# Block attention and MoE layer on one core: the column softmax's weights turned on VectorE instead of TensorE, sread in 32x64 tiles

## The chip, the cores and the metric

The kernel runs on one core of a Trainium2 chip. The metric is device time in microseconds of one execution; the median of three runs is given. A profile shows one execution of the program.

## The reference

Two stages are chained. The first is an attention between 512 tokens `x` and 32 state rows per head, for 8 batches of 8 heads with 64 elements. The scores are used twice: a softmax along the states (rows) gives `xread`, a softmax along the tokens (columns) gives `sread`.

```python
# x: (8, 8, 512, 64), state: (8, 8, 32, 64), all float32
scores = scale * x @ state^T                      # 512 x 32
xread  = softmax(scores, -1) @ state              # 512 x 64
scores2 = scale * state @ x^T                     # 32 x 512
sread  = softmax(scores2, -1) @ x                 # 32 x 64
attn = concatenate([xread, sread], axis=2)        # 544 rows per batch and head
# second stage, on rows of H*D = 512 elements
h = attn_rows @ w_in                              # 512 -> 2048
r = maximum(h, 0); g = s * (r * r) + b
out = g @ w_out                                   # 2048 -> 512, 4352 rows
```

## The kernel before, in words

There are no loops over stages. `ORDER` (lines 15 to 75) is a list of words, and lines 713 to 716 emit the piece that each word names, in that order, on the engine that the piece uses. An argument `V`, `A` or `G` puts a piece on VectorE (DVE), ScalarE (ACT) or GpSimd (POOL). Each engine works its own instructions strictly in this order, so a piece whose input is late holds back everything behind it on its engine. DMAs of inputs are issued from POOL's queue (x, weights; line 217 to 220 from ACT, line 214 from SyncE), those of outputs from SyncE's.

A batch b (8 of them, number 0 in two halves p at the start) goes through these pieces:

- `x` (load_x, L177): both head groups g of four heads, tokens laid out so that a partition holds 16 successive tokens of a head, converted to 16 bits. `xn` (load_xn, L188): the same data in a second layout for sread. Batch 0 comes as `xf` by SyncE in four parts (L210) and is cast by `castx`.
- `xT` (L283): DVE turns 32x32 blocks. `T` (L291): the scores by 16 matmuls of 32x32 weight tiles and 512 columns. `U`, `mu`, `D`, `E1`, `z`, `At`, `A` (L312 to 358): the row softmax, whose result `A` is again turned on DVE.
- `M` (L423) multiplies the states with w_in, eight matmuls of 64x32 tiles for each quarter j; `Mc` copies it to SBUF. So layer 1 of xread is `l` or `lh` (L469, L473): two matmuls of 512 columns with `M` and `A`, then a relu on ACT. `s`, `sh` square it.
- `L` (L492), a quarter of layer 2 for 128 rows: four matmuls of 512 columns; `out` adds the bias and stores. Batches 5 to 7 use a Strassen-like scheme instead: sums `S` of blocks, 14 half products `P`, evictions `ev`, stores `put`.
- The column softmax: `nm`, `nms` (maximum over the tokens), `E2` (L374, exp on ACT), `a2` (L381, scaling by the reciprocal sum on DVE, written in another order of the tokens). `aps` (L391) turns it with eight TensorE transposes of 128x128 into PSUM, `a2T` (L397) copies that to SBUF on ACT or DVE, and `V` (L400) multiplies with `xn`: 32 matmuls of 128x64 weights and 32 columns a batch, one PSUM bank, two batches together in two of the calls. `srd` (L420) copies the result to `srdT` on ACT.
- At the end `lsr`, `ssr`, `S_sr`, `P_sr`, `ev_sr` do both layers for the sread rows of all batches.

PSUM has eight banks: two rooms of two banks (`two_banks`, L130: `ps_t` with own=1, `ps_a` with own=0), which `T`, `M`, `aps`, `V` and a few others take in turn, two single banks for layer 1 and two for layer 2. `idle` (L656) are matmuls on constants at the start. All small matmuls go through the helper `mm` and so have line L137 in the profile.

Of the kernel before, what the change touches and what calls it, by code (L numbers as in the profile page):

```python
# [78 lines left out]
def kernel(  # L79
# [90 lines left out]
    srdT = konst.tile([P, NK, Ns, B], FP16, name="srdT")  # L170
# [5 lines left out]

    def load_x(b):  # L177

        if b > 2:
            nc.gpsimd.tensor_copy(ahead, at[b - 1]["xT"][0:1, 0, 0])  # L180
        xh_t[b] = xpool.tile([P, NG, NT, D], FP16, name=f"xh_{b}", tag="xh")
        for g in range(NG):
            nc.gpsimd.dma_start(
                out=xh_t[b][:, g].rearrange("p j d -> p (j d)"),
                in_=x[b, 4 * g : 4 * g + 4].rearrange("r (t j) d -> (r t) (j d)", j=NT),
            )

    def load_xn(b):  # L188

        xn_t[b] = xpool.tile([P, H, SCH, D], FP16, name=f"xn_{b}", tag="xn")  # L190
        for jh in range(4):
            nc.gpsimd.dma_start(  # L192
                out=xn_t[b][32 * jh : 32 * jh + 32].rearrange("t h c d -> t h (c d)"),
                in_=x[b].rearrange("h (t jh c) d -> jh t h (c d)", t=32, jh=4)[jh],
            )
# [15 lines left out]
    for p in range(2):  # L211
        for g in (1, 0):
            h = slice(NT // 2 * p, NT // 2 * p + NT // 2)
            nc.sync.dma_start(
                xf[g][:, h], x[0, 4 * g : 4 * g + 4].rearrange("r (t j) d -> (r t) j d", j=NT)[:, h]
            )
# [174 lines left out]
    def at_aps(b):  # L391
        at[b]["aps"] = aps = blocks(two_banks(f"aps_{b}", FP16), 0)
        for g in range(NG):
            for c in range(SCH):
                transp(aps[:, SCH * g + c], at[b]["a2"][:, g, P * c : P * c + P])
# [351 lines left out]
```

## Time and profile before

| | |
|---|---|
| median of 3 runs | 224.83 us (224.76 to 225.58) |
| the profiled execution | 224.36 us |
| its span in the profile | 222.2 us |
| instructions in the profile | 4473 |
| granted TensorE clock | full speed in all 40 slices |
| DMA | 22.67 MB in 23416 packets |
| `l`: two matmuls of 512 columns, then the relu (L456) | 0.61 us on ACT |
| copy `srdT` (L421), 128x128 | 0.73 us on ACT (median) |
| `a2` (L385), 128x512 | 0.35 us on DVE |
| `A` turned (L353), 128x512 pairs | 0.71 us on DVE |
| `aps` copied (L152) | 1.02 us on ACT, 0.67 us on DVE |
| square of 128x1024 | 0.68 us on DVE, 1.08 us on ACT |
| product of 128x512 on POOL (L462) | 1.06 us |

An engine's busy time is the time in which at least one of its instructions ran; a matmul's duration contains its latency, so that successive matmuls overlap and what one costs is read from start to start. PE is TensorE's matmuls, PEld its weight loads, L the line of the kernel, and a name such as `vps<-a2T,xn` says which tile is written from which.

### The profile page before, as it was taken

Reading aid. Unit: us, or ns where it says so; the run is one execution under the profiler, and the core shown is the slowest. Engines: PE = TensorE matmul, PEld = TensorE weight load, DVE = VectorE, ACT = ScalarE, POOL = GpSimd, SP = SyncE. Lnnn points to the kernel's source line nnn. Section 1 sums busy time; section 2 is a strip of 40 time slices with the busy share of each in tenths; the row PEclk is TensorE's granted clock in tenths of the full one; section 3 lists DMA queues with packets and bytes.
Section 4 is the critical chain, followed back from the end, with each engine's and each line's share of the span. In section 5 each row is a group of like instructions: output and inputs, shape, how many; then the busy total and the mean of one; then the engine's idle time right before and its main releaser. Section 6 shows DMA issues by size and latency. Waiting matters only on the chain.

```text
span 222.2 us, 4473 instructions
## 1 busy us (share of the span) xinstructions
PE 210.7 (95%) x1816; PEld 115.8 (52%) x1816; DVE 183.6 (83%) x267; ACT 141.8 (64%) x243; POOL 43.4 (20%) x73
## 2 busy tenths in 40 slices
PE   6469999999999999999999999999999999999992
PEld 2234334444444443444454544457766778888881
DVE  1597998889769997989796799889999997966772
ACT  2475895776488869855787479485877858533400
POOL 8245504000273400046002160005200000000000
PEclk9999999999999999999999999999999999999999
DMA  6999993420557892048927397226903500440066
GB/s 158 227 207 206 205 193 58 101 72 20 100 112 117 112 174 50 16 100 120 192 47 133 96 128 124 49 45 101 141 2 65 127 0 3 94 99 0 3 134 149
DMA packets 23416, 22.67 MB, mean 102 GB/s; under 512 B 4196, under 2 KB 16996, under 8 KB 23396
## 3 DMA queue, kind: packets, MB, share of 16 engines
q0 software_dynamic: 16560, 12.26, 38.6%
q1 hardware_dynamic: 6160, 9.97, 18.2%
q8 instruction: 14, 0.23, 0.4%
q10 hardware_dynamic: 676, 0.16, 0.3%
q14 instruction: 6, 0.05, 0.1%
HBM read 25.72 MB, written 8.91 MB: 156 GB/s over the span
## 4 chain that ended last, share of the span: by engine, by line
PE 88%; DMA 4%; DVE 3%; ACT 3%; SPq 1%; issue 0%
PE ops L496 31%; PE hps L452 24%; PE opf_X L137 9%; PE opf_W L137 5%; PE mps L137 4%; DMA xf<-in_x_dram 4%; PE hps_sr L452 3%; PE opf_Y L137 2%; PE vps L137 2%; PE T_None L137 2%; PE aps L137 2%; PE ops_sr_X L137 2%; ACT M L152 1%; DVE xT L289 1%; PE ops_sr_W L137 1%; ACT rh L482 1%
## 5 line engine op out<-in xcount | busy, mean ns | idle before, releaser
L456 ACT ACTIVATE r<-hps 128x512 f16<-128x512 f32 x120 | 69.3, 610 | 29.8 <-PE hps L452 28.4
L496 PE MATMUL ops<-w_out,g 128*128 128x512 f16 x320 | 78.1, 379 | 1.3 <-DVE g L462 1.3
L452 PE MATMUL hps<-A,M 128*128 128x512 f16 x240 | 65.3, 380 | 0.5 <-DVE M L152 0.3
L496 PEld LDWEIGHTS <-g 128*128 128x128 f16 x320 | 30.3, 98 | 38.4 <-issue 2.8
L462 DVE TENSOR_TENSOR g<-r 128x1024 f16<-128x1024 f16 (+1 forms) x39 | 34.5, 897 | 8.1 <-ACT r L456 8.0
L452 PEld LDWEIGHTS <-M 128*128 128x128 f16 x240 | 21.9, 98 | 25.8 <-issue 4.7
L137 PEld LDWEIGHTS <-g 128*128 128x128 f16 x288 | 28.0, 98 | 6.4 <-issue 0.2
L152 ACT CAST M<-mps 128x1024 f16<-128x1024 f32 x28 | 28.0, 1013 | 1.8 <-PE mps L137 1.8
L192 POOL DMA_DIRECT2D xn<-in_x_dram x32 | 18.5, 588 | 29.2 <-PE vps L137 28.3
L506 DVE SCALAR_TENSOR_TENSOR osb<-ops,sb_bc,bias_bc 128x512 f32<-128x512 f32 x20 | 14.7, 734 | 1.0 <-PE ops L496 1.0
L180 POOL COPY ahead<-xT 1x2 f16<-1x2 f16 x5 | 1.8, 367 | 67.0 <-DVE xT L289 67.0
L456 ACT ACTIVATE r_sr<-hps_sr 128x256 f16<-128x256 f32 x16 | 6.2, 385 | 12.8 <-PE hps_sr L452 12.4
L564 DVE TENSOR_TENSOR g<-g 128x1024 f16<-128x1024 f16 x18 | 12.2, 685 | 2.0 <-PE opf_Y L137 1.9
L289 DVE STREAM_TRANSPOSE xT<-xh 128x1024 f32<-128x1024 f32 (+2 forms) x12 | 10.3, 871 | 3.2 <-ACT xh L152 3.2
L333 DVE TENSOR_REDUCE z<-E 128x32 f32<-128x1024 f16 (+1 forms) x9 | 9.9, 1095 | 3.7 <-ACT E L328 3.7
L137 PE MATMUL opf_X<-w_T,g 128*128 128x256 f16 x96 | 11.9, 273 | 0.0
L137 PE MATMUL mps<-w_in,stT 64*32 64x512 f16 x256 | 11.2, 383 | 0.2 <-ACT M L152 0.2
L318 DVE TENSOR_REDUCE mu<-U 128x32 f32<-128x1024 f32 (+1 forms) x9 | 9.9, 1097 | 0.2
L376 ACT ACTIVATE E<-T_None,nms 128x512 f16<-128x512 f32 x8 | 5.5, 691 | 6.9 <-DVE nms L372 4.4
L328 ACT ACTIVATE E<-Dm 128x1024 f16<-128x1024 f32 (+1 forms) x9 | 8.7, 963 | 1.8 <-DVE Dm L322 1.5
L322 DVE TENSOR_TENSOR Dm<-U,mu 128x1024 f32<-128x1024 f32 (+1 forms) x8 | 9.6, 1201 | 0.2
L314 DVE STREAM_TRANSPOSE U<-T_None 128x1024 f32<-128x1024 f32 x7 | 8.7, 1247 | 1.2 <-PE T_None L137 0.8
(94 smaller groups left out, 259.4 us busy)
## 6 DMA issues: line engine op xcount, KB each, us to landing
out_dram<-osb SPq DMA_DIRECT2D x32, 128.0 KB, 2.7
xn<-in_x_dram POOLq DMA_DIRECT2D x32, 128.0 KB, 5.7
xh<-in_x_dram POOLq DMA_DIRECT2D x14, 256.0 KB, 5.2
out_dram<-osx SPq DMA_DIRECT2D x24, 128.0 KB, 2.4
w_in<-in_moe_w_in_dram POOLq DMA_DIRECT2D x8, 256.0 KB, 10.6
w_out<-in_moe_w_out_dram POOLq DMA_DIRECT2D x4, 512.0 KB, 12.7
xf<-in_x_dram SPq DMA_DIRECT2D x4, 256.0 KB, 7.5
out_dram<-osb SPq DMA_DIRECT2D x4, 256.0 KB
```

The lines of the kernel that those rows point to most:

```text
L137: return nc.tensor.matmul(out, lhsT, rhs, start=start, stop=stop, tile_position=tp, is_transpose=is_transpose, skip_group_check=skip,)
L152: (engine.copy if engine is nc.scalar else engine.tensor_copy)(out, in_)
L192: nc.gpsimd.dma_start(out=xn_t[b][32 * jh : 32 * jh + 32].rearrange("t h c d -> t h (c d)"), in_=x[b].rearrange("h (t jh c) d -> jh t h (c ...
L289: nc.vector.transpose(part(out, p, g), part(in_, p, g))
L318: nc.vector.tensor_reduce(part(mu, p), blk(part(at[b]["U"], p)), AX.X, ALU.max)
L333: nc.vector.tensor_reduce(part(z, p), blk(part(at[b]["E1"], p)), AX.X, ALU.add)
L452: nc.tensor.matmul(hps, lhsT, rhs, start=(i == 0), stop=(i == len(terms) - 1))
L456: nc.scalar.activation(R_t[tag, q][:, i], hps, AF.Relu)
L462: e.tensor_mul(g, r, r)
L496: nc.tensor.matmul(ops_t[tag, rr], G_t[tag][:, f, P * rr : P * rr + P], w_out_f(f), start=(f == 0), stop=(f == NKF - 1),)
L506: nc.vector.scalar_tensor_tensor(osb, ops_t.pop((tag, rr)), s_bc, bias_bc, ALU.mult, ALU.add)
L564: e.tensor_tensor(out, x, y, op)
```

## The change

The two copies of a batch's tokens are laid out anew. `x_u` splits the 512 tokens into halves u of 256; a partition holds eight successive tokens of each half (four DMAs a batch for two). `xn` gets the layout that the first copy had: 16 successive tokens of a head in a partition, in three DMAs for four. `T` reads its columns in the order (v u t), so that the scores and all that follows from them for the column softmax are in that order, and `a2` writes straight on. `aps` is gone; `a2T` is one DVE instruction that turns 32x32 blocks of pairs within SBUF. `V` has 128 matmuls a batch: 16 steps j, in each the eight tiles of 32 rows by 64 columns (four row groups hp, two column groups g), which write into four banks, that is both rooms. `srd` copies from the two rooms with one instruction each, to an `srdT` whose last axis is now the states. The output's row patterns follow the new layouts. Pieces may take a whole (index 2 of `HALVES`) where they took a half, tiles for the relu's results are given out in turn, and `ORDER` is written anew throughout, with other engines for many pieces.

```diff
 ORDER = [
-    "win.0 win.1 wout.0 x.1 win.2 wout.1 win.3 wout.2 wout.3 idle.11 castx.1.0.V castx.0.0.A xT.0.0.0 "
-    "casts.A turn.0.4.A pair.0.4 xT.0.1.0 T.0.1.0 U.0.0 mu.0.0 sb castx.1.1.A castx.0.1.A D.0.V.0 "
-    "xT.0.0.1 idle.6 xT.0.1.1 E1.0.0 T.0.0.1 keep.0.0 M.0.0.1 Mc.0.0.A z.0.0 At.0.V.0 A.0.0 idle.4 "
...
+    "x.1 casts.V pair.0.4 castx.0.0.V castx.1.0.A xT.0.0.0 turn.0.4.A xT.0.1.0 T.0.1.0 U.0.0 mu.0.0 "
+    "D.0.V.0 castx.1.1.A xT.0.1.1 E1.0.0 castx.0.1.V xT.0.0.1 keep.0.0 idle.8 win.0 M.0.0.1 z.0.0 "
+    "Mc.0.0.A T.0.0.1 keep.0.1 idle.4 win.1 idle.2 At.0.V.0 A.0.0 U.0.1 lh.0.2.0 mu.0.1 wout.0 D.0.V.1 "
+    "lh.0.0.0 M.0.1.0 Mc.0.1.A win.2 E1.0.1 win.3 sh.0.2.0.V M.1.0.1 sb Mc.1.0.A lh.0.4.0 lh.0.6.0 "
...
+    "L.2.0.2 l.2.15 l.2.14 L.2.3.0 L.2.3.1 l.3.2 l.3.5 V.3 srd.3 l.3.3 s.2.14.2.G L.2.0.3 out.2.0 l.3.8 "
...
+    "out.2.1 V.4 srd.4 l.3.4 s.3.4.4.V T.5.1 l.3.12 l.3.11 nm.5 s.3.0.4.A L.2.3.2 L.2.2.0 nms.5.A L.2.2.1 "
...
+    "L.3.2.2 L.3.2.3 out.3.2 V.2 s.4.2.2.V srd.2 l.4.14 V.5 srd.5 L.3.3.3 l.4.10 l.4.15 out.3.3 s.4.0.2.V "
...
-    srdT = konst.tile([P, NK, Ns, B], FP16, name="srdT")
+    srdT = konst.tile([P, NK, B, Ns], FP16, name="srdT")
+    def x_u(b, g, u):
+        return x[b, 4 * g : 4 * g + 4].rearrange("r (u t v) d -> u r t v d", u=2, t=32)[u]
...
-        for g in range(NG):
+        for g, u in np.ndindex(NG, 2):
             nc.gpsimd.dma_start(
-                out=xh_t[b][:, g].rearrange("p j d -> p (j d)"),
-                in_=x[b, 4 * g : 4 * g + 4].rearrange("r (t j) d -> (r t) (j d)", j=NT),
+                out=xh_t[b][:, g, NT // 2 * u : NT // 2 * u + NT // 2].rearrange("p v d -> p (v d)"),
+                in_=x_u(b, g, u).rearrange("r t v d -> r t (v d)"),
             )
...
-        for jh in range(4):
+        for g, k, n in ((0, 0, 4), (1, 0, 2), (1, 2, 2)):
+            h = 4 * g + (k ^ 2 * g)
             nc.gpsimd.dma_start(
-                out=xn_t[b][32 * jh : 32 * jh + 32].rearrange("t h c d -> t h (c d)"),
-                in_=x[b].rearrange("h (t jh c) d -> jh t h (c d)", t=32, jh=4)[jh],
+                out=xn_t[b][32 * k : 32 * k + 32 * n, g].rearrange("p j d -> p (j d)"),
+                in_=x[b, h : h + n].rearrange("r (t j) d -> (r t) (j d)", j=NT),
             )
...
+    def in_order(t, p, turned):
+        if p is not None:
+            return t
+        if turned:
+            return t.rearrange("q (u v t) -> q v u t", u=2, t=32)
+        return t.rearrange("q (v u t) -> q v u t", u=2, t=32)
     def at_T(b, own=1, p=None):
...
-                    r = hp ^ g
+                    r = hp ^ 2 * g
                     mm(
-                        part(T[Ns * hp : Ns * hp + Ns], p, g)[:, 0, :],
+                        in_order(part(T[Ns * hp : Ns * hp + Ns], p, g)[:, 0, :], p, False),
                         stE[32 * r : 32 * r + 32, NG * b + g, :, e],
-                        part(at[b]["xT"][32 * r : 32 * r + 32, :, :, e], p, g)[:, 0, :],
+                        in_order(part(at[b]["xT"][32 * r : 32 * r + 32, :, :, e], p, g)[:, 0, :], p, True),
...
-            nc.vector.tensor_scalar(
-                a2[:, g].rearrange("p (c jh t) -> p jh c t", c=4, jh=4),
-                at[b]["E2"][:, g].rearrange("p (jh c t) -> p jh c t", c=4, jh=4),
-                q[:, g : g + 1], None, ALU.mult,
-            )
-    def at_aps(b):
-        at[b]["aps"] = aps = blocks(two_banks(f"aps_{b}", FP16), 0)
-        for g in range(NG):
-            for c in range(SCH):
-                transp(aps[:, SCH * g + c], at[b]["a2"][:, g, P * c : P * c + P])
-    def at_a2T(b, e):
-        copy(e, sm(b, "a2T", [P, NG * SCH, P], FP16, apool, 2), at[b]["aps"])
-    def at_V(*bs):
-        pair = two_banks(f"vps_{bs[0]}")
...
+            nc.vector.tensor_scalar(a2[:, g], at[b]["E2"][:, g], q[:, g : g + 1], None, ALU.mult)
+    def at_a2T(b):
+        a2T = sm(b, "a2T", [P, NG, NT // 2, Ns, 2], FP16, apool, 2)
+        nc.vector.transpose(
+            a2T.rearrange("p g v n e -> p (g v n e)").bitcast(FP32),
+            at[b]["a2"].rearrange("p g s -> p (g s)").bitcast(FP32),
+        )
+    def at_V(b):
+        pair = at[b]["vps"] = [two_banks(f"vps_{b}_{i}", own=i) for i in range(2)]
+        a2T, xn = at[b]["a2T"], xn_t[b]
+        for j in range(NT):
+            e, v = j // (NT // 2), j % (NT // 2)
+            for hp in range(4):
                 for g in range(NG):
...
+                    r, rows = hp ^ 2 * g, slice(32 * hp, 32 * hp + 32)
+                    mm(
+                        pair[r // 2][D * g : D * g + D, r % 2, :Ns],
+                        xn[rows, g, j, :],
+                        a2T[rows, g, v, :, e],
+                        start=(j == 0),
+                        stop=(j == NT - 1),
+                        tp=(32 * hp, D * g),
+                    )
     def at_srd(b):
-        nc.scalar.copy(srdT[:, :, :, b], at[b]["vps"])
+        for i in range(2):
+            nc.scalar.copy(srdT[:, 2 * i : 2 * i + 2, b], at[b]["vps"][i][:, :, :Ns])
```

More of the change, by code (lines that the diff above doesn't have):

```diff
@@ L181, in load_x @@
         xh_t[b] = xpool.tile([P, NG, NT, D], FP16, name=f"xh_{b}", tag="xh")
-        for g in range(NG):
+        for g, u in np.ndindex(NG, 2):
             nc.gpsimd.dma_start(
-                out=xh_t[b][:, g].rearrange("p j d -> p (j d)"),
-                in_=x[b, 4 * g : 4 * g + 4].rearrange("r (t j) d -> (r t) (j d)", j=NT),
+                out=xh_t[b][:, g, NT // 2 * u : NT // 2 * u + NT // 2].rearrange("p v d -> p (v d)"),
+                in_=x_u(b, g, u).rearrange("r t v d -> r t (v d)"),
             )
     def load_xn(b):
-        xn_t[b] = xpool.tile([P, H, SCH, D], FP16, name=f"xn_{b}", tag="xn")
-        for jh in range(4):
+        xn_t[b] = xpool.tile([P, NG, NT, D], FP16, name=f"xn_{b}", tag="xn")
+        for g, k, n in ((0, 0, 4), (1, 0, 2), (1, 2, 2)):
+            h = 4 * g + (k ^ 2 * g)
             nc.gpsimd.dma_start(
-                out=xn_t[b][32 * jh : 32 * jh + 32].rearrange("t h c d -> t h (c d)"),
-                in_=x[b].rearrange("h (t jh c) d -> jh t h (c d)", t=32, jh=4)[jh],
+                out=xn_t[b][32 * k : 32 * k + 32 * n, g].rearrange("p j d -> p (j d)"),
+                in_=x[b, h : h + n].rearrange("r (t j) d -> (r t) (j d)", j=NT),
             )
@@ L214 @@
             nc.sync.dma_start(
-                xf[g][:, h], x[0, 4 * g : 4 * g + 4].rearrange("r (t j) d -> (r t) j d", j=NT)[:, h]
+                xf[g][:, h].rearrange("p v d -> p (v d)"), x_u(0, g, p).rearrange("r t v d -> r t (v d)")
             )
@@ L376, in at_E2 @@
         nc.scalar.activation(
-            E2[:, g], scores(b)[:, g], AF.Exp,
+            in_order(E2[:, g], None, False), in_order(scores(b)[:, g], None, b == 0), AF.Exp,
             bias=at[b]["nms"][:, g : g + 1], scale=scale, accum_out=rs[:, g : g + 1],
@@ L397, in at_a2T @@
-    def at_a2T(b, e):
-        copy(e, sm(b, "a2T", [P, NG * SCH, P], FP16, apool, 2), at[b]["aps"])
-    def at_V(*bs):
-        pair = two_banks(f"vps_{bs[0]}")
-        for v, b in enumerate(bs):
-            vps = pair[:, v, : NK * Ns].rearrange("p (k n) -> p k n", n=Ns)
-            a2T, xn = at[b]["a2T"], xn_t[b]
-            for k in range(NK):
-                for g in range(NG):
-                    hp = k ^ g
-                    for i in range(SCH):
-                        mm(
-                            vps[D * g : D * g + D, k, :],
-                            xn[:, 4 * g + k, i, :],
-                            a2T[:, SCH * g + i, Ns * hp : Ns * hp + Ns],
-                            start=(i == 0),
-                            stop=(i == SCH - 1),
-                            tp=(0, D * g),
-                        )
-            at[b]["vps"] = vps
+            nc.vector.tensor_scalar(a2[:, g], at[b]["E2"][:, g], q[:, g : g + 1], None, ALU.mult)
@@ L427, in at_M @@
             for g in range(NG):
-                r = hp ^ g
+                r = hp ^ 2 * g
                 mm(
@@ L447, in new_G, with in_turn @@
         return G_t[tag]
+    turns = {}
+    def in_turn(shape, name, tag, n):
+        k = turns[tag] = turns.get(tag, -1) + 1
+        return rpool.tile(shape, FP16, name=name, tag=f"{tag}{k % n}", bufs=1)
     def layer1(tag, f, terms, ntok):
@@ L454, in layer1 @@
         if (tag, q) not in R_t:
-            R_t[tag, q] = rpool.tile([P, 4, ntok], FP16, name=f"r_{tag}_{q}", tag="r")
+            R_t[tag, q] = in_turn([P, 4, ntok], f"r_{tag}_{q}", "r", 3)
         nc.scalar.activation(R_t[tag, q][:, i], hps, AF.Relu)
@@ L480, in layer1_half @@
                 mm(hps[:, i, :], lhsT, part(A, p, g)[:, 0, :], start=(g == 0), stop=(g == NG - 1))
-        r = R_t[b, f, p] = rpool.tile([P, 2, HALF], FP16, name=f"rh_{b}_{f}_{p}", tag="rh", bufs=4)
+        r = R_t[b, f, p] = in_turn([P, 2, HALF], f"rh_{b}_{f}_{p}", "rh", 4)
         nc.scalar.activation(r, hps, AF.Relu)
@@ L487, in layer1_sr @@
     def layer1_sr(f):
-        layer1("sr", f, [(w_in_f(k, f), srdT[:, k].rearrange("p n b -> p (n b)")) for k in range(NK)], B * Ns)
+        layer1("sr", f, [(w_in_f(k, f), srdT[:, k].rearrange("p b n -> p (b n)")) for k in range(NK)], B * Ns)
     ops_t = {}
@@ L514, in out_x @@
         if b:
-            store(b, rr, rows.rearrange("(t r i e) n -> r i t e n", r=SCH, i=2, e=2)[rr], 2)
+            store(b, rr, rows.rearrange("(u t r i) n -> r i t u n", u=2, r=SCH, i=2)[rr], 2)
         else:
-            store(b, rr, [rows.rearrange("(t r j) n -> r j t n", r=SCH, j=4)[rr]])
+            store(b, rr, [rows.rearrange("(u t r j) n -> u r j t n", u=2, r=2, j=4)[rr // 2, rr % 2]])
+    HALVES = (slice(0, 4), slice(4, 8), slice(0, 8))
     fast_w = {}
@@ L525, in weight_sum @@
             fast_w[name] = konst.tile([P, NKF // 2, HALF], FP16, name=f"w_{name}", tag=f"w_{name}")
-        w = w_out16[:, 8 * h : 8 * h + 8]
-        B = [[w[:, k::2, HALF * n : HALF * n + HALF] for n in range(2)] for k in range(2)]
-        T = {k: t[:, 4 * h : 4 * h + 4] for k, t in fast_w.items()}
+        w = w_out16
+        B = [[w[:, k::2, HALF * n : HALF * n + HALF][:, HALVES[h]] for n in range(2)] for k in range(2)]
+        T = {k: t[:, HALVES[h]] for k, t in fast_w.items()}
         a, b = {
@@ L555, in act_sum @@
     def act_sum(b, name, h, e):
-        A = lambda i, j: block(b, i, j)[:, 4 * h : 4 * h + 4]
+        sl = HALVES[h]
+        A = lambda i, j: block(b, i, j)[:, sl]
         out, x, y, op = {
@@ L560, in act_sum @@
             2: lambda: (A(0, 0), A(1, 0), A(0, 0), ALU.subtract),
-            3: lambda: (fast(b, "S3")[:, 4 * h : 4 * h + 4], A(0, 0), A(1, 0), ALU.subtract),
+            3: lambda: (fast(b, "S3")[:, sl], A(0, 0), A(1, 0), ALU.subtract),
             4: lambda: (A(0, 1), A(0, 1), A(0, 0), ALU.subtract),
@@ L598, in put @@
         t = fast(b, str(i))[:, rr]
-        rows = out_BSn[b, 0:S].rearrange("(t r i e) n -> r i t e n", r=SCH, i=2, e=2)[2 * i + rr]
+        rows = out_BSn[b, 0:S].rearrange("(u t r i) n -> r i t u n", u=2, r=SCH, i=2)[2 * i + rr]
         for n in range(2):
             nc.sync.dma_start(rows[n], t[64 * n : 64 * n + 64])
-    out_sr = out_BSn[:, S:ST, :].rearrange("b (r t) n -> r t b n", r=2)
+    out_sr = out_BSn[:, S:ST, :].rearrange("(r b) t n -> r b t n", r=2)
     def sr_block(i, j):
@@ L620, in sum_sr @@
         }[name]
-        out, x, y = (t[:, 4 * h : 4 * h + 4] for t in (S_sr(name), x, y))
+        out, x, y = (t[:, HALVES[h]] for t in (S_sr(name), x, y))
         e.tensor_tensor(out, x, y, op)
@@ L706 @@
         "E1": at_E1, "z": at_z, "At": at_At, "A": at_A, "nm": at_nm, "nms": at_nms, "E2": at_E2, "a2": at_a2,
-        "aps": at_aps, "a2T": at_a2T, "V": at_V, "srd": at_srd, "M": at_M, "Mc": at_Mc,
+        "a2T": at_a2T, "V": at_V, "srd": at_srd, "M": at_M, "Mc": at_Mc,
         "lh": layer1_half, "sh": square_half, "l": layer1_x, "s": square, "lsr": layer1_sr,
```

108 rows, old and new, of the table ORDER are left out of this document.

## The prediction

> **What bounds the kernel now.** First the page's totals and its chain of waits:
>
> ```profile
> PE 210.7 (95%) x1816; PEld 115.8 (52%) x1816; DVE 183.6 (83%) x267; ACT 141.8 (64%) x243; POOL 43.4 (20%) x73
> ...
> PE 88%; DMA 4%; DVE 3%; ACT 3%; SPq 1%; issue 0%
> ```
>
> TensorE (PE) is busy nearly throughout, and the end is released along it. Then the windows, to see whether that holds in every stage (duration, then busy time of each engine):
>
> ```profile
> 15.00:30.00 15.00, 12.94 (x111) 5.43 (x110) 13.15 (x17) 11.92 (x20) 6.80 (x8) 1.00 1.22 206
> ...
> 60.00:90.00 30.00, 30.00 (x232) 13.18 (x231) 26.11 (x36) 25.07 (x41) 8.76 (x12) 1.00 0.65 112
> ...
> 150.00:180.00 30.00, 30.00 (x321) 20.61 (x319) 29.05 (x41) 20.56 (x35) 4.57 (x8) 1.00 0.51 81
> ```
>
> From 60 us PE has no idle time at all, from 30 to 60 us 0.22. Its list of waits sums to 7.2 us, nearly all of it in the first 30. So after the start, a microsecond of matmul work taken away or added is a microsecond of the kernel, as long as the other engines keep up; before 30 us the DMA (about 200 GB/s without a break) and the chain of the first batch decide.
>
> **What the change takes from PE.** The timeline of PE around one column softmax (start, busy time, instruction):
>
> ```profile
> 87.59 0.41 PE L137 MATMUL mps<-w_in,stT 64*32 64x512 f16 x8
> 87.93 1.04 PE L496 MATMUL ops<-w_out,g 128*128 128x512 f16 x4
> 88.81 0.61 PE L137 MATMUL aps<-ident,a 128*128 128x128 f16 x8
> 89.25 0.59 PE L496 MATMUL ops<-w_out,g 128*128 128x512 f16 x2
> ...
> 99.94 0.64 PE L137 MATMUL T_None<-xT,stE 32*32 32x512 f16 x16
> 100.51 0.71 PE L137 MATMUL vps<-a2T,xn 128*64 128x32 f16 x32
> 101.14 0.60 PE L452 MATMUL hps<-A,M 128*128 128x512 f16 x2
> ...
> 126.05 1.21 PE L137 MATMUL vps<-a2T,xn 128*64 128x32 f16 x64
> 127.19 0.60 PE L452 MATMUL hps<-A,M 128*128 128x512 f16 x2
> ```
>
> Read from start to next start. The eight transposes (`aps`) hold PE 89.25 - 88.81 = 0.44 us, in each of 8 batches 3.5 us. sread (`vps`) holds it 0.63 us, and in a pair 1.14 us, so 32 further matmuls add 0.51 us: **15.9 ns each**. Four single V and two pairs give 4 x 0.63 + 2 x 1.14 = 4.8 us. About 0.1 us of each run is the change of the array's tile shape: `mps` holds 0.34 us, where one stream of 512 columns is 0.21 and seven further starts 0.03. I count these changes apart: 6 x 0.1 off leaves 4.2 us. Together **7.7 us** go, or 0.97 us a batch.
>
> **What it adds to PE.** A batch now has 16 x 4 x 2 = 128 matmuls of 32x64 weights and 32 columns, where there were 32. The trace has no such matmul, so I bound it. Below: `mps` starts eight matmuls in different tiles within 0.41 - 0.386 = 0.024 us (one takes 386 ns in its group), 3.4 ns apart, weight loads beside them; 128 x 3.4 = 0.43 us. If weight loads and matmuls took turns at 3.4 ns, 0.87 us. Above: if tiles bring no overlap, V's own 15.9 ns, 128 x 15.9 = 2.03 us. The nearest rows are `mps` and `T`, in which several tiles do run together; but there the queue held the instructions ready, and 256 of them at once are not seen. I take the middle of the lower two, **0.65 us**, 5.2 us in all: 5.2 - 7.7 = **-2.5 us** (-4.3 at 0.43, -0.7 at 0.87, +8.5 at 2.03; zero at 0.97).
>
> [...]
>
> Counted in the two written orders, PE changes tile shape 72 times before and 71 after: -0.1 us. The permuted reading in `at_T` moves the same 512 columns; I cost it at nothing (its matmuls already read every second element), with no row for another price.
>
> **New waits of PE.** V now takes both two-bank rooms, which T and M use too, and frees them by two copies of 64 columns (`at_srd`). Rows: a copy of 128 columns with scattered writes 0.73 us, of 256 dense ones 0.37, of 2 columns 0.16; I take 0.22. A room is free about 0.25 (last matmul's duration, and a start of U 0.07 us after T's end) + 2 x 0.22 + 0.2 = 0.9 us after V's last start. What lies on PE between V and the next user of the rooms, by the order: V.3, V.5, V.0, V.6 and V.7 have 0.86 us or more (layer-1 pieces at 0.43, layer-2 quarters at 0.86). V.4 has only l.3.4 before T.5.1, V.2 only l.4.14 before V.5: 0.43 + 0.1 of shape change. Two waits of 0.9 - 0.5: **+0.7 us** (nothing if the copies start at once and T's place is freed early; 2.8 if a copy stays at 0.73). Behind a waiting T.5.1 stand all later matmuls, so it is paid in full.
>
> **The other engines.** DVE gets eight transposes of 128x512 pairs (`A`, 0.71 us: +5.7) and loses four evictions of `aps` (0.67: -2.7); ACT loses four (1.02: -4.1) and pays one more start a batch for `srd`. The scaling `a2` (0.35 us) writes straight on now; a gain of at most 2 x 0.2 us a batch on DVE. The new order moves far more: squares on ACT go from 3 to 21, arithmetic on POOL from 5 pieces to 31. With the rows' means (POOL 128x512 1.06 us, so about 2.1 for 1024) DVE has some 25 us less, ACT 14 more, POOL 55 more. ACT then comes to about 155 busy us of 222 and DVE to about 160, both under PE; none is on the path by its total. POOL's arithmetic has a price for DVE:
>
> ```profile
> 24.17 2.11 DVE L322 TENSOR_TENSOR Dm<-U,mu 128x1024 f32<-128x1024 f32 x1
> 26.20 0.41 DVE L462 TENSOR_TENSOR g<-rh 128x512 f16<-128x512 f16 x1
> ```
>
> The first took 1.22 us elsewhere; a product ran on POOL beside it (24.16, 1.04 us). With 55 us of POOL work and a fifth of the time in such two-input pieces on DVE, about 11 us fall on DVE: within the 25 that it gained.
>
> **The start.** ACT and DVE here (before):
>
> ```profile
> 10.36 0.62 ACT L152 CAST xh<-xf 128x512 f16<-128x512 f32 x1 [1.38 <-DMA xf<-in_x_dram]
> 10.89 0.62 ACT L328 ACTIVATE E<-Dm 128x512 f16<-128x512 f32 x1
> ...
> 11.71 0.64 DVE L333 TENSOR_REDUCE z<-E 128x16 f32<-128x512 f16 x1
> ```
>
> E stands behind a cast that waits for DMA, though Dm was done at 9.6. The new order puts E before that cast and the cast on DVE, before z: z can start at 10.36 + 0.47 (cast) + 0.40 (turn) = 11.2, 0.5 us earlier. Against it x.1, four issues on POOL's queue (0.56 us each), now goes ahead of win.0: half a megabyte, 2.5 us at 200 GB/s. POOL waited for a w_in landing until 8.78, so win.0 comes at about 11.3, just before M needs it (12.18); the last weights move by no more, since the bytes are the same, and xn's transfers (three for four a batch, longer rows) come later. **-0.5 us**, from -1.5 (all that E gains) to +1.0 (weights last). The end (4 us from the last matmul to the span's end) stays.
>
> **Sum.** -2.5 - 0.1 + 0.7 - 0.5 = -2.4 us. The profiled execution took 224.36 us (span 222.2 and 2.2 around it), so 222.0; the median of the runs shown is 0.47 above it, so **222.4**.
>
> **Rivals.**
> - *Small matmuls don't overlap* (place: V on PE; it decides from 0.97 us a batch). Eight weight tiles may load one after another, or PE's queue may not be fed 256 instructions at such a rate: V's 64 matmuls showed 15.9 ns throughout. For it: no row is faster over more than some 32 instructions. Against it: `T` and `mps` tiles. At 2.03 us: 222.4 + 11.0 = 233.4; half way 228. Chance 0.26. [...]
> - *The gain is lost in waits*: the rooms closed by V, ACT (whose pieces come to about 20 us by the rows' means beside the 20 us of PE work after the first 30), or POOL's pieces late for a matmul. Eight batches at 0.3 us give back 2.4: 224.8. For it: the two thin places; against it, PE without idle under a DVE at 29.05 of 30 us. Chance 0.18.
> - *POOL slows DVE in one stage* (150 to 180 us, where DVE was at 97%): 3 us more there, 225.4. Chance 0.06.
> - Forecast: 0.50.
>
> **Numbers.** Low end: 0.43 us a batch, start -1.5, no waits: -4.3 - 0.1 - 1.5 = -5.9, 218.9. High end 230: V at about 1.6 us a batch; beyond it lies some 0.1. A run of this kernel can tell about 0.5% (1.1 us) from no change. Faster than 223.7: the forecast's case, 0.50. Slower than 225.9: the first rival and half of the third with part of the second, 0.33. Between: 0.17.
>
> **What would show it.** V in the timeline of PE: 0.5 to 0.75 us from start to next start confirms the main term, over 1.07 (0.97 and the shape change) refutes it. T.5.1 and V.5 waiting for ACT's `srdT` confirm the two waits. `lh` first at about 13.7 instead of 14.16 confirms the start. Idle time of PE after 30 us with other releasers, ACT `r` or POOL above all, would mean the second rival. Wrong altogether: PE no longer the chain's main part.

## The result, and the profile after

The changed kernel took **255.14 us** (median of 4 runs, 253.06 to 257.61), the kernel before 224.80 in the same job: ratio **1.131**, interval 1.125 to 1.138. I had forecast 222.4, and no more than 230.0 in 8 cases of 10. The profiled execution took 253.06 us; its span is 251.1, 28.9 more than before. A ratio leaves out executions that fell in a slower state (here the one of 257.61 us), so it can differ from the quotient of the two medians.

The page of the kernel after, totals and chain of waits:

```profile
PE 215.0 (86%) x2513; PEld 117.5 (47%) x2513; DVE 166.3 (66%) x234; ACT 150.4 (60%) x264; POOL 100.4 (40%) x105
...
PE 68%; DMA 15%; DVE 6%; POOL 5%; issue 1%; ACT 1%; POOLq 0%; DVEq 0%; ACTq 0%
```

PE is busy 4 us longer than before; the other 25 of the 29 us are time in which it stands. The chain gives them to DMA (15%, before 4%). The windows of the same kernel (duration, then busy time of PE, PEld, DVE, ACT and POOL, the granted clock, DMA share, GB/s) say where:

```profile
15.00:30.00 15.00, 9.03 (x57) 2.97 (x57) 9.04 (x16) 3.12 (x5) 5.62 (x8) 0.79 0.94 145
...
60.00:90.00 30.00, 26.77 (x175) 10.75 (x174) 22.48 (x28) 20.00 (x32) 18.04 (x20) 0.94 0.49 84
150.00:180.00 30.00, 29.95 (x441) 14.93 (x439) 24.56 (x38) 22.38 (x38) 15.29 (x21) 1.00 0.69 121
```

From 150 us to the last matmul PE is full again, and DVE is even freer. The loss lies in the start, at single places of the middle, and at the end. DVE's two casts of batch 0 (timeline; start, busy time, instruction, idle time before it):

```profile
15.28 0.60 DVE L152 CAST xh<-xf 128x512 f16<-128x512 f32 x1 [11.56 <-DMA xf<-in_x_dram]
...
23.60 0.56 DVE L152 CAST xh<-xf 128x512 f16<-128x512 f32 x1 [3.11 <-DMA xf<-in_x_dram]
```

The four parts of xf are cast at 6.56, 15.28, 19.39 and 23.60 us; before at 3.64, 5.29, 8.37 and 10.36. So the first `lh` (layer 1) starts at 29.47 instead of 14.16, and the first layer-2 matmul at 33.84 instead of 16.55. On POOL:

```profile
14.89 0.77 POOL L211 DMA_DIRECT2D w_out<-in_moe_w_out_dram  x1 [8.12 <-DMA xh<-in_x_dram]
19.11 0.62 POOL L205 DMA_DIRECT2D w_in<-in_moe_w_in_dram  x1 [3.44 <-DMA xh<-in_x_dram]
```

x.1 now has four issues, w_in four behind them, and the ninth issue, w_out's, stands until the first of the eight lands. (Before, the ninth issue of the queue, w_in's at 8.78, waited in the same way for the first w_in.) In the trace each of the first eight issues has a semaphore of its own, and the ninth names the first one's again and waits for it: the eight belong to the program, and no run here shows a limit of the queue itself. Then PE at 60 us and around V.5:

```profile
63.32 0.64 PE L137 MATMUL T_None<-xT,stE 32*32 32x512 f16 x16 [2.76 <-DVE xT L294]
...
136.70 1.21 PE L137 MATMUL vps<-a2T,xn 32*64 32x32 f16 x128
137.84 0.60 PE L465 MATMUL hps<-A,M 128*128 128x512 f16 x2
138.38 1.26 PE L137 MATMUL vps<-a2T,xn 32*64 32x32 f16 x120
141.54 0.22 PE L137 MATMUL vps<-a2T,xn 32*64 32x32 f16 x8 [1.90 <-issue]
```

T.3 waits for batch 3's x, and seven matmuls behind it take 427 ns instead of 216: the granted clock is 0.50 from 64.72 us on, for 3.41 us. (In these traces it is 1.00 or, for 3.41 us or a multiple and at the end, 0.50.) A V holds PE 137.84 - 136.70 = 1.14 us (four of the eight do; three others take 1.35 to 1.53); V.5 stands 1.90 us before its last eight matmuls, waiting for nothing that the profile shows ("issue"). Last, the end: the last matmul starts at 242.43, the span ends at 251.1, 8.7 us later; before it was 222.2 - 217.86 = 4.4. Behind it there are only one sum on DVE and the landing of the four stores of the state rows. These are issued as fast as before (after, then before), but now SP waits for their landing, 5.0 us in its list of waits, 1.2 before:

```profile
242.26 2.47 SPq L714 DMA_DIRECT2D out_dram<-osr  x4
```

```profile
217.00 2.51 SPq L699 DMA_DIRECT2D out_dram<-osr  x4
```

### The profile page after: what moved, and what is told of

The parts are those of the page before. It is cut to its first block, busy times and chain, and to the rows that moved or that the text cites. A ratio compares the mean times of both kernels' runs of the same rounds, so it can differ in the third digit from the quotient of the medians.

```text
span 251.1 us, 5888 instructions
## 1 busy us (share of the span) xinstructions
PE 215.0 (86%) x2513; PEld 117.5 (47%) x2513; DVE 166.3 (66%) x234; ACT 150.4 (60%) x264; POOL 100.4 (40%) x105
## 3 DMA queue, kind: packets, MB, share of 16 engines
q1 hardware_dynamic: 6064, 9.97, 15.9%
## 4 chain that ended last, share of the span: by engine, by line
PE 68%; DMA 15%; DVE 6%; POOL 5%; issue 1%; ACT 1%; POOLq 0%; DVEq 0%; ACTq 0%
PE ops L509 20%; PE hps L465 17%; PE opf_X L137 8%; DMA w_in<-in_moe_w_in_dram 8%; PE opf_W L137 4%; DMA xn<-in_x_dram 4%; PE vps L137 4%; DMA xh<-in_x_dram 3%; POOL xh L187 3%; PE hps_sr L465 3%; PE mps L137 3%; PE opf_Y L137 2%; PE ops_sr_X L137 1%; PE hph L137 1%; PE dps L675 1%
## 5 line engine op out<-in xcount | busy, mean ns | idle before, releaser
L475 POOL TENSOR_TENSOR g<-r 128x1024 f16<-128x1024 f16 x12 | 23.9, 2002 | 23.5 <-ACT r L469 23.5
L473 ACT ACTIVATE g<-r 128x1024 f16<-128x1024 f16 (+1 forms) x21 | 25.2, 1219 | 0.7 <-PE ops L509 0.6
L152 ACT CAST M<-mps 128x1024 f16<-128x1024 f32 x21 | 21.3, 1013 | 6.5 <-PE mps L137 6.5
L187 POOL DMA_DIRECT2D xh<-in_x_dram x28 | 19.5, 700 | 4.6 <-DMA w_in<-in_moe_w_in_dram 2.3
L335 POOL TENSOR_TENSOR Dm<-U,mu 128x1024 f32<-128x1024 f32 x4 | 8.0, 2002 | 29.2 <-DVE mu L331 29.2
L475 DVE TENSOR_TENSOR g<-r 128x1024 f16<-128x1024 f16 (+1 forms) x21 | 16.4, 795 | 4.8 <-ACT r L469 4.8
L137 PE MATMUL mps<-w_in,stT 64*32 64x512 f16 x256 | 11.8, 389 | 5.5 <-DMA w_in<-in_moe_w_in_dram 4.6
L197 POOL DMA_DIRECT2D xn<-in_x_dram x24 | 13.2, 566 | 6.4 <-PE vps L137 6.4
L152 DVE CAST M<-mps 128x1024 f16<-128x1024 f32 x11 | 13.4, 1214 | 2.5 <-PE mps L137 2.4
L137 PE MATMUL vps<-a2T,xn 32*64 32x32 f16 x1024 | 10.7, 192 | 2.0 <-issue 1.9
L356 POOL TENSOR_TENSOR At<-E,rz 128x1024 f16<-128x1024 f16 x3 | 5.7, 1911 | 15.9 <-DVE rz L347 11.0
```

The lines of the kernel that those rows point to most:

```text
L137: return nc.tensor.matmul(out, lhsT, rhs, start=start, stop=stop, tile_position=tp, is_transpose=is_transpose, skip_group_check=skip,)
L152: (engine.copy if engine is nc.scalar else engine.tensor_copy)(out, in_)
L187: nc.gpsimd.dma_start(out=xh_t[b][:, g, NT // 2 * u : NT // 2 * u + NT // 2].rearrange("p v d -> p (v d)"), in_=x_u(b, g, u).rearrange("r ...
L197: nc.gpsimd.dma_start(out=xn_t[b][32 * k : 32 * k + 32 * n, g].rearrange("p j d -> p (j d)"), in_=x[b, h : h + n].rearrange("r (t j) d -> ...
L473: nc.scalar.activation(g, r, AF.Square)
L475: e.tensor_mul(g, r, r)
```

## The experiments

Ratios are against the kernel before in the same job; "us" of a difference is the difference of two ratios times 225 us.

**Where the transfers' shape comes in.** The change reads x with the heads as the outermost of three dimensions (4 x 32 rows), where before (r t) was one dimension of 128. The page's lines on the two queues, first of the kernel before, then after:

```profile
q0 software_dynamic: 16560, 12.26, 38.6%
q1 hardware_dynamic: 6160, 9.97, 18.2%
```

```profile
q0 software_dynamic: 23056, 12.30, 36.5%
q1 hardware_dynamic: 6064, 9.97, 15.9%
```

SP's queue (q1) moves the same 9.97 MB with 96 packets fewer. The missing ones are of 4 bytes: 8 transfers have this shape (xf's four loads and the state rows' four stores; below, undoing either brings 48 back), 96 / 8 = 12 each. The semaphores show the same: that of an xf transfer has sixteen late updates before and four after, besides a single one soon after the issue. And of the 512 packets of 2 KB that bring xf, up to 19 are under way at one time before; after, it is four during 12.1 of the 20.4 us that they take, and never more than six. That four of the 16 engines carry such a transfer is my reading of these counts: the trace doesn't say which engine a packet took. The packets of data on this queue are the same in number and size, 4,608 of 2 KB and 512 of 1 KB, so smaller pieces are not the reason.

*e3: x_u alone, on the kernel before* (V, order and end as before; the tokens of each batch stand in another order):

```diff
-        for g in range(NG):
+        for g, u in np.ndindex(NG, 2):
...
-                in_=x[b, 4 * g : 4 * g + 4].rearrange("r (t j) d -> (r t) (j d)", j=NT),
+                in_=x_u(b, g, u).rearrange("r t v d -> r t (v d)"),
```

> The kernel before, with its order and its matmuls, in which only the loads of x take the changed kernel's form (two halves of 256 tokens, four heads outermost; the tokens then stand in another order, so rows of the output are permuted within a head). Theory A: the four xf transfers land at 6, 13, 18 and 23 us or later, where they landed at 3.6 to 10.4, the first layer-1 matmul moves from 14.2 to 25 us or later, and the time rises by 10 to 20 us, to 235 to 245 us. Theory B (the order is to blame): the time stays within 2 us of 224.8.

242.96 us, ratio 1.077 [1.072, 1.082]: +17.4 us, theory A. The casts come at 7.92 to 26.41, the first `lh` at 31.38; the end stays at 4.3 us.

*e1: x by heads, on the kernel after* (each transfer 32 partitions of one head; q1 has 6,304 packets, 16 x 16 - 4 x 4 = 240 more than after, so sixteen reports for each of xf's transfers):

```diff
-        for g, u in np.ndindex(NG, 2):
+        for g, r in np.ndindex(NG, 4):
...
-                in_=x_u(b, g, u).rearrange("r t v d -> r t (v d)"),
+                in_=x[b, 4 * g + r].rearrange("(u t v) d -> t u (v d)", u=2, t=32),
```

> The changed kernel, in which only the loads of x in the new layout are issued one head at a time, so that the outermost dimension of each transfer is 32 tokens' rows and not 4 heads (8 transfers a batch for 4, 16 for 4 for batch 0). Theory A (the transfers with an outermost dimension of 4 run on 4 of the 16 DMA engines, and that delays the start): the first layer-1 matmul, at 29.5 us in the changed kernel, comes at 14 to 17 us, the wait for batch 3's x at 60 us goes with the slow clock behind it, and the time falls by 15 to 20 us, to 233 to 238 us. Theory B (the new order puts x.1 ahead of the weights and is late for that reason, whatever the transfers' shape): the first layer-1 matmul stays behind 25 us and the time falls by less than 5 us. Under A the semaphore packets of each of the four xf transfers are 16, not 4.

255.26 us, 1.133 [1.127, 1.139]: nothing gained, so theory B by its total. But the first `lh` came 8.1 us earlier (21.36, where B had said behind 25), and that was lost again: 5.7 us from 32.0 on, where PE waited for ACT's `rh`, the rest behind it and at 59 us. What holds `rh` up is shown below.

*e2: the same, with the stores divided* (`out_x` of batch 0 in four, the state rows' in four on two queues):

```diff
-            nc.sync.dma_start(out_sr[i][:, :, sl], out[:, sl])
+            for k in range(4):
+                (nc.sync, nc.scalar)[k % 2].dma_start(out_sr[i][k][:, sl], out[32 * k : 32 * k + 32, sl])
```

> As the run before, and the stores of batch 0 and of the sread rows are also issued one head group row at a time, from 32 partitions each (outermost dimension 32 for 4), those of sread from two queues. Theory A: the time from the last matmul to the end of the span falls from 8.4 us to about 4 us (4.0 in the kernel before), and the total by another 3.5 to 4.5 us, to 229 to 234 us. Theory B: the tail is the four stores' own issue and completion, and stays above 7 us.

248.81 us, 1.103 [1.098, 1.108]: 6.7 us less than by heads alone, but far above A. From the last matmul to the end 6.4 us (9.0 by heads alone), between the theories' numbers.

*e5: x as before, on the kernel after.* V's pairs need an order of columns; ACT's exponent of the column softmax can write it, and then x's layout need not change. Loads, T and `out_x` as before:

```diff
-            in_order(E2[:, g], None, False), in_order(scores(b)[:, g], None, b == 0), AF.Exp,
+            E2[:, g].rearrange("q (v t e) -> q e v t", e=2, t=32),
+            scores(b)[:, g].rearrange("q (e v t) -> q e v t", e=2, t=32), AF.Exp,
```

> The kernel after with x loaded as before (two transfers a batch, 128 partitions as one dimension); the exponent writes its columns in the order that V's pairs need instead, so V, the new order and the stores of the state rows stay, and all outputs are computed. Theory A (the transfers' shape: x by heads keeps few DMA engines and holds POOL's queue, in which a ninth issue waits for the first to land): first lh at 13.5 to 15, no wait for xh at 60 us, 232 to 239 us; the last matmul 8 to 9 us before the end, as after. Theory B (the new order with its work on ACT and POOL costs the time, wherever x comes from; splitting x by heads brought the start 8 us forward and no gain): above 245 us, with PE waiting for ACT or POOL between 25 and 65 us.

234.94 us, 1.043 [1.039, 1.047]: **-19.8 us**, theory A. T.3 no longer waits; the end stays at 8.6 us. The first `lh` comes at 16.41, later than A's 13.5 to 15. The exponent takes 0.83 to 0.92 us in this order, 0.68 to 0.74 before.

*e6: and the state rows as before* (the columns of srdT in the old order):

```diff
-    out_sr = out_BSn[:, S:ST, :].rearrange("(r b) t n -> r b t n", r=2)
+    out_sr = out_BSn[:, S:ST, :].rearrange("b (r t) n -> r t b n", r=2)
```

The outermost dimension of each store is 16 now, where it was 4.

> The run above, and the state rows' columns and stores as before (16 engines for each store instead of 4). Theory A: 4 us less than the run above, 228 to 235 us, and 4 to 4.5 us from the last matmul to the end. Theory B: the end is set by the amount that is stored; less than 1 us of difference.

231.3 us, 1.029 [1.025, 1.033]: **-3.2 us**; 230.5 - 225.42 = 5.1 us from the last matmul to the end, for 8.6. Theory A, a little less than it said.

**Why more transfers cost.** *e11: x by heads on e7* (e7, below, is e6 with V.5 moved), the layout unchanged:

```diff
-        for g in range(NG):
+        for g, r in np.ndindex(NG, 4):
...
-                in_=x[b, 4 * g : 4 * g + 4].rearrange("r (t j) d -> (r t) (j d)", j=NT),
+                in_=x[b, 4 * g + r].rearrange("(t j) d -> t (j d)", j=NT),
```

> The run with V.5 apart, with each batch's x loaded by heads: eight transfers of 32 partitions where there were two of 128, the same layout, rows of 4 KB, 16 engines. Theory A: POOL's ninth issue waits for the first to land, so the products and the scaling behind x.2 and x.3 on POOL come late: 4 to 15 us more than the run with V.5 apart, PE waiting for work of ACT or POOL between 20 and 60 us. Theory B: six more issues of 0.54 us a batch (some 23 us on POOL) lie beside other work: under 2 us.

247.62 us, 1.099 [1.094, 1.104]: **+18.7 us** for six more issues a batch, more than A expected. Its timeline of POOL, ACT and PE, one fence each:

```profile
31.77 0.49 POOL L187 DMA_DIRECT2D xh<-in_x_dram  x1 [0.79 <-DMA stn<-in_state_dram]
34.36 0.49 POOL L187 DMA_DIRECT2D xh<-in_x_dram  x1 [2.10 <-DMA w_out<-in_moe_w_out_dram]
34.95 3.04 POOL L476 TENSOR_TENSOR g<-rh 128x512 f16<-128x512 f16 x3
```

```profile
36.04 0.60 ACT L496 ACTIVATE rh<-hph 128x512 f16<-128x512 f32 x1 [8.73 <-POOL g L476]
```

```profile
36.69 1.86 PE L466 MATMUL hps<-A,M 128*128 128x512 f16 x4 [8.64 <-ACT rh L496]
```

The issues of x.2 are spread from 21.7 to 34.9 us, all but the first behind an earlier landing. The squares stand behind them on POOL's queue; ACT has no free `rh` until the first is done; PE has no free `hps` until ACT is. That is where e1's 8 us went as well (there PE waits 5.75 us for the same `rh` at 37.74). Besides, in e11 the granted clock is 0.50 for 6.83 us from 32.72 on, and T.3 waits 3.44 us for x.3.

**Which of the two queues.** From e7, too, x_u again for one kind of load alone: xf on SP's queue (e13), xh on POOL's (e14). The tokens of batch 0, then of batches 1 to 7, stand in another order.

> The run with V.5 apart, with batch 0's four loads alone (xf, on SP's queue) in the form of the change, heads outermost; the tokens of batch 0 then stand in another order. Theory A (four engines carry each of these transfers, so 256 KB take some 4 us one after another, and batch 0's chain waits for them): casts at about 6.5, 11, 15 and 19, first lh 6 to 10 us later, 6 to 10 us more than the run with V.5 apart. Theory B (the many small packets of POOL's transfers in this form are what holds the start up, in xf's way too): under 2 us.

245.99 us, 1.092 [1.085, 1.098]: **+17.1 us**, twice what A expected. Casts at 7.89, 16.77, 23.29 and 29.00, first `lh` at 33.05: some 7 us for each 256 KB, 37 GB/s.

```profile
16.77 0.43 DVE L152 CAST xh<-xf 128x512 f16<-128x512 f32 x1 [13.08 <-DMA xf<-in_x_dram]
```

> The run with V.5 apart, with the loads of batches 1 to 7 alone (xh, on POOL's queue, four transfers a batch for two) in the form of the change; the tokens of these batches then stand in another order. Theory A (each transfer carries some 400 small packets and a ninth issue waits for the first of eight to land): w_in comes late, first lh 4 to 8 us later, xh of batch 3 late at 40 to 60 us, 7 to 14 us more than the run with V.5 apart. Theory B (xf's few engines make the whole loss): under 3 us.

236.26 us, 1.044 [1.036, 1.053]: **+6.4 us**, just under A's lower end. The first w_out issue waits until 11.41 (4.79 us for an xh), but the first `lh` comes at 17.57, only 1.3 us later than in e7, where A said 4 to 8. T.3 waits for its x once more:

```profile
51.16 1.05 PE L137 MATMUL T_None<-xT,stE 32*32 32x512 f16 x16 [2.76 <-DVE xT L294]
```

e7 and e14 run the same matmuls in the same order. Matmul by matmul the profiled execution (238.26 us, the longest of its four) is 2 us behind e7's until T.3, and 7.7 behind it: 2.8 of wait and 3 at a granted clock of 0.50. These loads have 10,976 small packets more (15,044 under 512 B for 4,068), 392 for each of 28 transfers. What writes them, and whether they or the additional issues cost the 6.4 us, stays open. Together the two would be 23.5 us; in the kernel after they made 19.8 and on the kernel before 17.4 (e3), as waits that overlap would.

**V.** *e4: V's part alone, on the kernel before* (x as before, V moved ahead of T.4, T.5, T.6 and T.7; the sread rows get other tokens' weights):

> The kernel before with only the column softmax's part changed: weights turned by VectorE, sread in eight 32x64 tiles over four banks, the second copy of x in the three longer transfers; V stands ahead of T of the next batch where the order needs that. The tokens of the two factors of sread don't match, so the sread rows are other numbers. Theory A (V costs PE about 1.04 us and a shape change, 0.1 more than what it replaces, and PE's queue is fed at 8.4 ns for a weight load and a matmul): 8 x 0.1 plus two waits of V for the rooms of the V ahead of it (0.7 us each) and up to 2 us of missing instructions where two V follow each other: 226 to 230 us. Theory C (the column softmax's part is what costs the 30 us, by a lack of overlap or of instructions): over 235 us. Theory D (V at 0.65 us as in the forecast): 222 to 224.5 us.

240.00 us, 1.064 [1.058, 1.071]: +14.5 us, far above A, in the range that C gave. In the order of before two V stood side by side, V.5 V.2 and V.6 V.0. Of the second of the first pair:

```profile
128.82 0.89 PE L132 MATMUL vps<-a2T,xn 32*64 32x32 f16 x77 [0.34 <-ACT srdT L411]
131.62 0.63 PE L132 MATMUL vps<-a2T,xn 32*64 32x32 f16 x51 [1.91 <-issue]
```

Each pair held PE 5.6 us, the granted clock was 0.50 for 6.83 us behind each, and T behind a V waited for `srdT` (1.9 us in four waits). So V's price depends on what stands next to it.

*e7: V.5 six pieces further behind V.2* (on e6):

```diff
-    "... V.2 s.4.2.2.V srd.2 l.4.14 V.5 srd.5 L.3.3.3 l.4.10 l.4.15 out.3.3 s.4.0.2.V "
+    "... V.2 s.4.2.2.V srd.2 l.4.14 L.3.3.3 l.4.10 l.4.15 out.3.3 s.4.0.2.V V.5 srd.5 "
```

> The run above with V.5 moved behind six further pieces (2.6 us of matmuls) after V.2. Theory A (512 instructions in 3 us are more than the instruction queue brings): V.5 loses its 2 us of idle time and the lower clock behind it, 2 to 3.5 us less than the run above. Rival (V.5 waits for the rooms or for its weights): the idle time goes with V.5, under 1 us of difference.

228.90 us, 1.016 [1.010, 1.021]: **-3.0 us**, theory A. V.5 still held PE 2.62 us (3.27 in e6), of which 0.69 "issue"; the greater part of the gain is the granted clock, 0.50 for 3.41 us behind V.5 in e6 and 1.00 here.

*e9: the weights issued first, on e7; e10: that, and V.5 moved behind L.4.0.2, some 10 us further:*

```diff
-    "x.1 casts.V pair.0.4 ... win.0 ... win.1 ... wout.0 ...
+    "win.0 win.1 wout.0 x.1 win.2 wout.1 win.3 wout.2 wout.3 casts.V pair.0.4 ...
```

> The run with V.5 apart, with the weights and x.1 issued in the order of before (win.0, win.1, wout.0, x.1, ...). Theory A: x.1 ahead of the weights holds M.0.0 up (it waited 1.1 and 0.8 us for w_in; first lh at 16.3 where before had 14.2): first lh at 14 to 15, 1.5 to 3 us less than the run with V.5 apart, 226 to 227.5 us. Theory B: the start is set by the first batch's chain on DVE (z at 11.75 and 11.71 in the two kernels): under 0.7 us of difference.

> The run above with V.5 nine more layer pieces further from V.2. Theory A (the instruction queue's supply): V.5 still stood idle 0.87 and 0.76 us where it was 2.6 us behind V.2; here it costs 1.15 us as the others do, 1 to 2.5 us less than the run above. Rival: a V stands idle wherever the queue has been emptied by small instructions; the idle time stays above 1 us.

230.36 us (1.022 [1.018, 1.026]) and 230.07 (1.020 [1.017, 1.024]). With the weights first, `lh` starts at 12.82, earlier than in any other kernel here, and the 3.5 us are gone again by 21 us:

```profile
12.82 1.03 PE L137 MATMUL hph<-A,M 128*128 128x256 f16 x8
...
21.23 0.63 PE L137 MATMUL mps<-w_in,stT 64*32 64x512 f16 x7 [1.95 <-DMA w_in<-in_moe_w_in_dram]
```

The last weights set this start, and the granted clock is 0.50 for 3.41 us behind this wait (not in e10, where PE waits for w_in five times, 3.2 us in all); V.3 begins at 82.6 us in the one kernel and 81.9 in the other. So A's mechanism holds and its gain doesn't. V.5 further away takes 1.15 us like the others, its idle time gone, as A said; of the 1.0 us that this takes off PE, the time of the kernel shows 0.3, within its interval. From V.3 to the last matmul it is 0.7 us shorter.

*e8: a quarter of V, on e6* (4 of 16 tokens in each row, so the sread rows lack the rest):

```diff
-        for j in range(NT):
+        for j in range(NT // 4):
...
-                        stop=(j == NT - 1),
+                        stop=(j == NT // 4 - 1),
```

> The second run of these (x and state rows as before) with V cut to a quarter: the matmuls of the first 4 of 16 tokens in each row alone (32 of 128 a batch), so the sread rows lack the rest. If V's matmuls hold PE 8.4 ns each after the first 32, 96 fewer a batch take 0.81 us off, 6.5 us in all, and some 2 to 4 us more where V.5 stalled: 7 to 10 us less. If V lay beside other work: under 2 us less.

220.20 us, 0.981 [0.976, 0.986]: **-10.9 us** against 231.3, a little over what was expected. The whole V holds PE 11.74 us in eight batches, the quarter 2.41, and the lower clock behind V.5 is gone too:

```profile
81.46 0.32 PE L137 MATMUL vps<-a2T,xn 32*64 32x32 f16 x32
81.85 0.59 PE L466 MATMUL hps<-A,M 128*128 128x512 f16 x2
```

*e12: V in two halves with a layer-1 or layer-2 piece between* (on e7; V.5 undivided):

```diff
-    V.3 srd.3 l.3.3
+    V.3.0 l.3.3 V.3.1 srd.3
...
-        for j in range(NT):
+        for j in range(8 * h, 8 * h + 8):
```

> The run with V.5 apart, with every V but V.5 in two halves of 64 matmuls and a layer-1 piece between them. If the first 32 matmuls run at 3 to 5 ns because they lie ready in a queue, and the rest at about 9 ns because they don't, the second half starts fast again: 64 matmuls in about 0.55 us, shape change included. If the slow rate belongs to the later matmuls as such (their operands, their accumulation), the second half takes 0.65 us or more, and 9 ns from its first matmul on.

Its timeline of V.3, and then the distances from start to start of the second half's matmuls, from the trace's records, in ns:

```profile
83.28 0.68 PE L137 MATMUL vps<-a2T,xn 32*64 32x32 f16 x64
83.89 0.60 PE L468 MATMUL hps<-A,M 128*128 128x512 f16 x2
84.42 0.68 PE L137 MATMUL vps<-a2T,xn 32*64 32x32 f16 x64
85.04 1.04 PE L512 MATMUL ops<-w_out,g 128*128 128x512 f16 x4
```

```
3 3 4 3 3 4 3 29 4 3 3 3 4 3 3 9 4 2 4 3 3 4 3 8 5 2 3 4 3 3 4   86
8 8 9 8 8 9 8 8 9 8 8 9 8 8 9 8 8 9 8 8 9 8 8 9 8 8 9 8 8 9 8
```

The second half starts fast again: 32 matmuls mostly 3 to 4 ns apart, then a pause, then 8.3 ns each, as in the first. So the slow rate doesn't belong to the later matmuls as such. That the first 32 matmuls, with their 32 weight loads, lay ready in a queue is my reading: the distances show where the rate changes, and no run shows the queue. A half costs 0.61 us, so nothing is gained by dividing: 232.09 us, 1.030 [1.026, 1.034], 3.2 us more than e7. V's hold is 1.4 us of this (12.4 for 11.1, with a wait of 1.0 for `srdT`); the rest stays open.

## Why the prediction was wrong, point by point

**The start: -0.5 us forecast, +15 to +17 measured.** This step failed. It counted bytes ("half a megabyte, 2.5 us at 200 GB/s", and "the last weights move by no more, since the bytes are the same") where in these runs the transfers' shape and number decided. xf, with four reports of its end for sixteen, came at 37 GB/s (e13: +17.1 us by itself). x.1's four slow transfers, with the four of w_in, took all eight of the program's semaphores on POOL's queue, but that cost the start only some 2 us (e14). That E goes ahead of a cast, the -0.5 us of the step, fits what was seen: with the weights first `lh` came 1.3 and 0.4 us earlier than before (e9, e10), though no run makes this move alone; M then waited for w_in, the +1.0 that the step had called "weights last".

No rival had this in it: the highest price among them was 233.4.

**The end: "stays" forecast, +4.3 measured.** The same reckoning by bytes failed once more: `out_sr` got an outermost dimension of 4. Undone, the end is 3.5 us shorter and the kernel 3.2.

**xh in the middle: not forecast.** At 60 us PE lost 2.76 us to batch 3's x, and 1.5 behind it to the lower clock. Both go with x's old loads (e5) and come back with xh's new ones alone (e14).

**V: the mechanism right, the size off.** Eight tiles do run together at 3 to 4 ns, but only for the first 32 matmuls. I had seen that no row was fast for longer than that, counted it for the first rival, and still taken 0.65 us from the middle of two bounds that both took 3.4 ns for all 128. Measured, where PE doesn't stand idle within a V: 1.145 - 0.1 = 1.04 us a batch against 0.97 that went. So the term is +0.6 us and not -2.5: **3.1 us** of error. The first rival, "PE's queue may not be fed 256 instructions at such a rate", fits what was measured, at its lower edge (it decided "from 0.97 us a batch").

**Two V in 3 us: not forecast.** PE stood idle within the second, 1.90 us after and 1.70 in e6, there with the lower clock behind it; 3.0 us in all (e7). The instruction queue of the page moved 19 blocks of 16 KB after, 14 before, 13 with a quarter of V: six fewer for 1,536 matmuls and weight loads. And in every trace in which PE stands longer than 0.2 us within a V for nothing that is named (nine runs, eleven times, up to 1.9 us), it goes on 1.2 to 1.4 us after such a block ended: after, the block takes from 138.66 to 140.12 and PE goes on at 141.54. That PE stands there for its instructions is read from these times alone; no run changes the blocks by themselves.

**The two waits for the rooms: +0.7 forecast, none measured.** The copies took 0.22 us each, as forecast, and PE's list of waits doesn't name `srdT`. (Where the copy scatters, in e6 and e7, it takes some 0.54 us, and PE waits 0.3 to 0.9 us.)

**Other engines: right.** DVE, ACT and POOL have 166, 150 and 100 busy us, and none of them bounds a stage from 90 us on; what POOL did to the path was its queue of issues, not its arithmetic.

The sum, by successive runs: after +29.5 us; x as before -19.8; state rows as before -3.2; V.5 apart -3.0; left +3.5. In the profiled executions 227.2 - 222.2 = 5.0 us are left: V's larger hold is 11.1 - 8.4 = 2.7 of them (its 8.4 before include the transposes), the end 5.1 - 4.4 = 0.7, and the rest, with a first `lh` 2.1 us later, isn't divided. No version that computes everything beat the kernel before: a V of 128 matmuls holds PE 1.145 us, the eight transposes and 32 matmuls 0.44 + 0.63 = 1.07.

## What to carry to other kernels

Before the bytes of a changed transfer are counted, look at its outermost dimension: with 4 there, a load of one megabyte came at 37 GB/s and the kernel lost 17 us (e13), and letting ACT's exponent write the order that was needed cost 0.15 us for each, off the critical path. Count the transfers in flight on a queue that also carries arithmetic: the program has eight semaphores for it, the ninth issue waited for the first landing (8.1 us in the kernel after), and everything behind it on that engine waited too. The 3 to 4 ns that the trace showed for a few small matmuls held here for the first 32 of a group; beyond that they cost 8.3 ns each, and where two groups followed each other PE stood up to 1.9 us.

## What the runs showed of the hardware

- V's matmuls (32x64 weights, 32 columns, eight tiles in turn) start mostly 3 to 4 ns apart for the first 32 of a group (4.5 on average) and 8.3 ns apart from then on, with a pause of 86 ns between; undisturbed, a group of 128 holds PE 1.145 us (after), one of 64 0.61 (e12), one of 32 0.25 (e8).
- Two such groups of 128 that start within 2 us left PE idle for 1.3 to 1.9 us (after, e1, e2, e4, e5, e6), 3.4 us apart for 0 to 0.7 (e7, e9, e11, e13, e14; without the wait for `srdT`), 7.4 us apart once for 0.9 (e4); 11.8 us apart (e10) they did not. PE went on 1.2 to 1.4 us after a 16 KB block of instructions had come.
- The granted clock fell to 0.50 for 3.41 us or a multiple, and matmuls of 512 columns took 427 ns instead of 216. It did so around 2.8 us of idle time (after, e14), after 1.7 us (e6) and after 1.3 us (e5), but not after the 1.9 us within V.5 in the kernel after, nor after 0.7 and 0.6 us in e7: the length of one idle time doesn't decide it.
- A copy of 128x64 out of PSUM on ACT took 0.22 us dense and 0.54 us (e7) where it scatters its columns (0.73 for 128x128 before).
- xf's loads of 256 KB landed 5.7 to 8.9 us apart with four reports of the end for each (e13) and 1.6 to 3.1 us apart with sixteen (before), each beside the weights' loads.
